# 64-row turns with shared banks, and a written-out order for all engines, in a lightning-attention and highway-FFN kernel

**Chip and metric.** One core of one Trainium2 chip. The time is device microseconds of one execution. "Fast" and "slow" are the two states in which executions fall; only fast runs are compared, and where a slow run or a slow profile is shown, it is said.

## The reference

Linear attention with a decay per head, in blocks of 64 tokens, then a highway feed-forward layer over all heads:

```python
# q, k, v: (4, 8, 768, 64) float32, lam: (8,), w_h, w_t: (512, 512), b_t: (512,)
for b in range(nb):                       # blocks of 64 tokens
    intra = einsum('bhic,bhjc->bhij', qb, kb) * Dmask      # lam ** (i - j), i >= j
    intra = einsum('bhij,bhjd->bhid', intra, vb)
    inter = einsum('bhid,bhde->bhie', qb * lam_pow, kv_state)
    out[:, :, sl] = intra + inter
    kv_state = lam_block * kv_state + einsum('bhsd,bhse->bhde', kb * rev_pow, vb)
x = out.transpose(0, 2, 1, 3).reshape(3072, 512)
H = maximum(x @ w_h, 0)
T = 1 / (1 + exp(-(x @ w_t + b_t)))
return T * H + (1 - T) * x                # float32, (3072, 512)
```

## The kernel before

It works in 12 stages of 256 tokens (J = 2 times 128 rows). In each stage k and q are loaded, scaled and turned, so that the head dimension lies on the partitions; scores, masks, state and output follow in 64x64 tiles; the feed-forward blocks come out transposed, and the result is turned back. The loads are issued by SyncE. Three functions concern us (the first serves k and q; the comments are mine):

```python
def trans(x, n, p, hs):              # k and q: 8 turns of 128 rows by 128 columns a group
    for i, h in enumerate(range(hs.start, hs.stop, 2)):
        for j in range(J):
            T.transpose(get(x + "tr", n, p)[:, i, j, :], get(x + "b", n)[:, j, h:h + 2, :], id128)
...
def block(x, w, g, js):              # feed-forward: 8 matmuls with 256 columns a call
    for i, j in enumerate(js):
        for kc in range(KC):
            T.matmul(get(x, g, js[0])[:, i, :], lhsT=w[:, kc, j * 128:(j + 1) * 128], rhs=get("xT", g)[:, kc, :],
                     start=(kc == 0), stop=(kc == KC - 1))
...
def turn(n, b, p, js):               # output: x + th, turned back; 8 turns of 128 rows
    g, r = group(n, b)
    for j in js:
        for i, x in enumerate(("xT", "th")):
            T.matmul(get("x", n, b, p)[:, (j - js[0]) * 128:(j - js[0] + 1) * 128],
                     lhsT=get(x, g)[:, j, r * C:(r + 1) * C], rhs=id128,
                     start=(j == js[0] and i == 0), stop=(i == 1), skip_group_check=True)
```

All of these write to tiles with the tag "w", which has three PSUM banks. Each piece of work is a task with an engine, a duration and a priority. At build time a planner simulates the engines and makes the order; among TensorE's candidates it ranks like this:

```python
k = (max(0.0, s - free[e] - GAP), (t.key if t.key > -9 else 99) + SAME * (t.mode != last_mode) + WAIT * (s - free[e]))
```

## Time and profile before

| | before |
|---|---|
| time, median of 3 | 116.28 us (115.97 to 116.59) |
| span in the trace | 113.2 us |
| TensorE busy | 101.2 us, 2145 matmuls in the trace |
| ScalarE / GpSimd / VectorE busy | 76.5 / 69.6 / 67.7 us |
| DMA | full until about 82 us |

TensorE is the bound in the middle, so the table is read from the top: another engine's busy time matters only where TensorE waits for it. The prediction below shows the lines. One line of the same page that it does not show turns out to be the important one, the queue that brings the instructions (packets, MB, share of the 16 DMA engines):

```profile
q8 instruction: 16, 0.26, 1.0%
```

(This trace, of 113.2 us, is of a fast run that took 115.21 us.)

### The profile page before, as it was taken

What the parts mean: (1) busy time and instruction counts of PE and PEld (TensorE: products, weight loads), DVE (VectorE), ACT (ScalarE), POOL (GpSimd) and SP (SyncE); (2) the same over time, 40 slices, a digit from 0 to 9 for tenths busy, and PEclk for the clock granted to TensorE, in tenths of its full rate; (3) what the DMA queues carried; (4) which work ended last, traced back from release to release, by engine and by line L of the source; (5) the groups of instructions that cost most, each with busy time, mean ns of one, the idle gap of its engine ahead of it and who ended that gap; (6) DMA issues with size and microseconds to landing.
All of it is one profiled execution on the core that took longest, in us unless ns stands there. A gap on an engine that the chain in (4) does not pass through costs nothing.

```text
span 113.2 us, 4880 instructions
## 1 busy us (share of the span) xinstructions
PE 101.2 (89%) x2145; PEld 88.9 (78%) x2145; DVE 67.7 (60%) x113; ACT 76.5 (68%) x146; POOL 69.6 (61%) x61
## 2 busy tenths in 40 slices
PE   4896576998897999999999999999999999998860
PEld 4895364778686788989889898998998989888750
DVE  0237756475266759658495676774966749764420
ACT  3595681556877676694879686967878667377550
POOL 6032337238999987979997997969597300404220
PEclk9999996799999999999999999999999999999999
DMA  0999999999999999999999999999951040403154
GB/s 9 255 298 291 311 329 349 302 263 300 279 296 291 336 352 306 293 288 298 307 320 310 285 340 294 333 285 298 337 184 53 11 180 6 184 7 148 37 208 162
DMA packets 43484, 27.57 MB, mean 243 GB/s; under 512 B 1348, under 2 KB 40520, under 8 KB 43464
## 3 DMA queue, kind: packets, MB, share of 16 engines
q1 hardware_dynamic: 43312, 27.27, 84.4%
q8 instruction: 16, 0.26, 1.0%
q14 instruction: 4, 0.03, 0.1%
q10 hardware_dynamic: 152, 0.01, 0.1%
HBM read 20.98 MB, written 6.29 MB: 241 GB/s over the span
## 4 chain that ended last, share of the span: by engine, by line
PE 72%; SPq 8%; DVE 7%; DMA 5%; ACT 3%; issue 2%; POOLq 1%; ACTq 0%
PE w L422 37%; PE w L444 9%; PE w L355 8%; SPq L341 7%; PE o L396 6%; DMA vf<-in_v_dram 5%; PE s L371 5%; PE o L384 5%; PE kv L404 4%; DVE m L375 3%; ACT w L435 2%; DVE xT L306 2%; DVE th L438 1%; SPq L300 1%; POOLq L602 1%
## 5 line engine op out<-in xcount | busy, mean ns | idle before, releaser
L422 PE MATMUL w<-xT,w_b 128*128 128x256 bf16 (+1 forms) x416 | 47.8, 267 | 1.4 <-DVE th L438 0.9
L422 PEld LDWEIGHTS <-w_b 128*128 128x128 bf16 x416 | 37.1, 99 | 6.5 <-issue 1.9
L375 DVE TENSOR_TENSOR m<-s,tri 128x512 bf16<-128x512 f32 x48 | 31.6, 686 | 14.7 <-PE s L371 14.7
L438 POOL TENSOR_TENSOR th<-t_sb,hmx 128x512 bf16<-128x512 bf16 (+1 forms) x13 | 14.0, 1080 | 21.2 <-DVE hmx L426 14.8
L349 POOL TENSOR_TENSOR qb<-qf,pow_q 128x1024 bf16<-128x1024 f32 (+1 forms) x13 | 22.1, 1703 | 7.8 <-DMA qf<-in_q_dram 7.7
L426 DVE SCALAR_TENSOR_TENSOR hmx<-w,xT 128x512 bf16<-128x512 f32 (+1 forms) x26 | 16.8, 647 | 10.0 <-PE w L422 5.2
L349 POOL TENSOR_TENSOR vs<-vf,pow_k 128x1024 bf16<-128x1024 f32 (+1 forms) x11 | 20.1, 1824 | 2.3 <-DMA vf<-in_v_dram 2.3
L450 ACT ACTIVATE o_sb<-w 128x512 f32<-128x512 f32 (+1 forms) x24 | 13.6, 587 | 5.3 <-PE w L444 5.0
L435 ACT ACTIVATE w<-w,bt_col 128x256 f32<-128x256 f32 (+1 forms) x26 | 11.2, 432 | 8.3 <-ACT kT L304 4.0
L304 ACT ACTIVATE qT<-w 128x1024 bf16<-128x1024 bf16 (+1 forms) x14 | 12.7, 904 | 4.8 <-PE w L355 4.8
L306 POOL CAST kb<-kf 128x1024 bf16<-128x1024 f32 (+1 forms) x11 | 11.0, 997 | 6.3 <-DMA kf<-in_k_dram 6.3
L304 ACT ACTIVATE kT<-w 128x1024 bf16<-128x1024 bf16 (+1 forms) x14 | 12.6, 896 | 1.9 <-PE w L355 1.9
L444 PE MATMUL w<-id,th 128*128 128x128 bf16 x96 | 12.9, 219 | 0.6 <-POOL th L438 0.6
L444 PE MATMUL w<-id,xT 128*128 128x128 bf16 x96 | 13.0, 220 | 0.4 <-DVE th L438 0.4
L438 DVE TENSOR_TENSOR th<-w,hmx 128x512 bf16<-128x512 f32 (+1 forms) x13 | 8.4, 645 | 6.3 <-ACT w L435 6.3
L435 ACT ACTIVATE t_sb<-w,bt_col 128x256 bf16<-128x256 f32 (+1 forms) x26 | 10.5, 461 | 2.4 <-PE w L422 2.4
L371 PE MATMUL s<-qT,kT 64*64 64x128 bf16 x384 | 11.4, 219 | 0.3 <-DVE m L375 0.3
L404 PE MATMUL kv<-vs,kb 64*64 64x64 bf16 x320 | 9.5, 197 | 1.3 <-POOL vs L349 0.9
L444 PEld LDWEIGHTS <-th 128*128 128x128 bf16 x96 | 9.3, 98 | 1.4 <-POOL th L438 0.8
L413 ACT ACTIVATE ss<-kv 128x256 bf16<-128x256 f32 x20 | 7.7, 384 | 3.5 <-PE kv L404 3.5
L404 PEld LDWEIGHTS <-kb 64*64 64x64 bf16 x320 | 8.0, 111 | 2.4 <-issue 1.6
L444 PEld LDWEIGHTS <-xT 128*128 128x128 bf16 x96 | 9.2, 98 | 0.5
(43 smaller groups left out, 109.2 us busy)
## 6 DMA issues: line engine op xcount, KB each, us to landing
out_dram<-o_sb SPq DMA_DIRECT2D x23, 256.0 KB, 4.9
kf<-in_k_dram SPq DMA_DIRECT2D x10, 512.0 KB, 7.5
qf<-in_q_dram SPq DMA_DIRECT2D x10, 512.0 KB, 7.8
vf<-in_v_dram SPq DMA_DIRECT2D x10, 512.0 KB, 7.0
kf<-in_k_dram SPq DMA_DIRECT2D x4, 256.0 KB, 5.2
qf<-in_q_dram SPq DMA_DIRECT2D x4, 256.0 KB, 5.7
vf<-in_v_dram SPq DMA_DIRECT2D x4, 256.0 KB, 6.1
w_f<-in_moe_w_h_dram SPq DMA_DIRECT2D x4, 256.0 KB, 6.2
```

Source lines behind the costliest of these rows:

```text
L304: A.activation(dst, src, AF.Copy)
L306: ENG[eng].tensor_copy(dst, src)
L349: ENG[eng].tensor_tensor(dst[:, hs], in0=get(x, n, p).rearrange("p h (j d) -> p h j d", j=J), in1=pw[:, :, :, None].to_broadcast([128, hs. ...
L371: T.matmul(get("s", n, u)[half(b), e, i, j, :], lhsT=get("kT", n)[half(e), hp, j, half(b)], rhs=get("qT", n)[half(e), hp, b * C:(b + 1) * ...
L375: V.tensor_tensor(get("m", n, u)[:, e], in0=get("s", n, u)[:, e], in1=tri[:, None].to_broadcast([128, 2, J, C]), op=ALU.mult)
L404: T.matmul(get("kv", n // NST)[half(e), hp, :], lhsT=get("kb", n)[half(b), j, 2 * hp + e, :], rhs=get("vs", n)[half(b), 2 * hp + e, j, :], ...
L422: T.matmul(get(x, g, js[0])[:, i, :], lhsT=w[:, kc, j * 128:(j + 1) * 128], rhs=get("xT", g)[:, kc, :], start=(kc == 0), stop=(kc == KC - 1))
L426: V.scalar_tensor_tensor(get("hmx", g, js[0]), in0=get("h", g, js[0]), scalar=0.0, in1=get("xT", g)[:, js[0]:js[-1] + 1, :], op0=ALU.max, ...
L435: A.activation(get(*gate(g, js))[:, i, :], get("t", g, js[0])[:, i, :], AF.Sigmoid, bias=bt_col[:, j:j + 1])
L438: ENG[TH[js[0] // 2]].tensor_tensor(get("th", g)[:, js[0]:js[-1] + 1, :], in0=get(*gate(g, js)), in1=get("hmx", g, js[0]), op=ALU.mult)
L444: T.matmul(get("x", n, b, p)[:, (j - js[0]) * 128:(j - js[0] + 1) * 128], lhsT=get(x, g)[:, j, r * C:(r + 1) * C], rhs=id128, start=(j == ...
L450: A.activation(get("o_sb", n, b, p), get("x", n, b, p), AF.Copy)
```

## The change

The intent is to make the turns cheaper. A turn of 128 rows by 128 columns becomes two turns of 64 rows by 64 columns, side by side in the two row halves of the array. Each group writes two banks, one for each row tile; k and q of a stage share these two, and so do the two halves of an output. Everything else is rearranged around that: the planner is gone, a list of 538 numbers gives the order of all tasks, and strings give the engine of each copy.

```diff
-def plan(tasks):
- ... (the whole planner, its durations and keys)
+EN = dict(cw="GVVGGVGV", ck2="AAAA", ..., ss="AAAAAAVVAAVVVAVVAVAV", eo="AAAVAAAAAAAAAAAVAAVAAV",
+          ck="GGGAGGGGGG", cq="VGGGGGGGGG", cv="VGGGGGGGGG", ...)
+ORDER = [44, 54, 20, 2, 21, 22, 23, 46, 24, ..., 520, 536, 537]
 ...
+    def trans2(i, n):
+        for hp in range(NP):
+            for j in range(J):
+                for b in range(2):
+                    T.transpose(get("tr", n, b)[:, i, hp, j, :], get("kq"[i] + "b", n)[half(b), j, 2 * hp:2 * hp + 2, :], id128[half(b), half(b)])
+    def evac2(n, b, eng):
+        copy(eng, get("kqT", n)[:, :, :, b * C:(b + 1) * C].rearrange("p x n (q j) -> p x n q j", j=J),
+             get("tr", n, b).rearrange("p x n j q -> p x n q j"))
 ...
+    def turn2(n, bs=(0, 1)):
+        for b in bs:
+            for j in range(NP):
+                for i, x in enumerate(("xT", "th")):
+                    for e in range(2):
+                        T.matmul(get("x", n, "e", e)[:, b, j, :], lhsT=get(x, n)[half(e), j, b * C:(b + 1) * C], rhs=id128[half(e), half(e)],
+                                 start=(b == 0 and j == 0 and i == 0), stop=(i == 1), skip_group_check=True)
 ...
-    for t in plan(tasks):
-        t.emit()
+    for i in ORDER:
+        t = tasks[i]
+        assert all(d in issued for d in t.deps)
+        issued.add(t)
+        t.emit(t.eng)
```

k and q of stages 2 to 11 and the output of stages 0 to 10 take the new form, 42 groups in all. The scores of the two halves of a head pair also get tiles of their own.

## The prediction

> **What bounds the kernel now.** I read the page first (busy shares and the 40 slices), then the groups of matmuls by form, the chain that ended last in order of time, and the timeline around single hand-overs.
>
> The page:
>
> ```profile
> PE 101.2 (89%) x2145; PEld 88.9 (78%) x2145; DVE 67.7 (60%) x113; ACT 76.5 (68%) x146; POOL 69.6 (61%) x61
> PE   4896576998897999999999999999999999998860
> POOL 6032337238999987979997997969597300404220
> PEclk9999996799999999999999999999999999999999
> DMA  0999999999999999999999999999951040403154
> ```
>
> TensorE is at 9 from slice 14 (about 40 us) to about 105 us. GpSimd is nearly full too, and the DMA is full, but only until about 82 us: both run ahead of TensorE and then stop. The clock dips only around 18 to 22 us. So the span is: a start in which the loads decide (0 to some 28 us), a long middle in which TensorE decides, and a tail. 113.2 us in this trace stand for 116.28 us of device time; I convert by that ratio.
>
> The matmuls by form (busy, mean ns, idle before):
>
> ```profile
> L422 PE MATMUL w<-xT,w_b 128*128 128x256 bf16 x352 | 43.8, 276 | 1.0 <-DVE xT L306 0.4 <-DVE th L438 0.4
> L444 PE MATMUL w<-id,xT 128*128 128x128 bf16 x96 | 13.0, 220 | 0.4 <-DVE th L438 0.4
> L444 PE MATMUL w<-id,th 128*128 128x128 bf16 x96 | 12.9, 219 | 0.6 <-POOL th L438 0.6
> L404 PE MATMUL kv<-vs,kb 64*64 64x64 bf16 x320 | 9.5, 197 | 1.3 <-POOL vs L349 0.9 <-ACT ss L413 0.4
> L355 PE MATMUL w<-id,qb 128*128 128x128 bf16 x96 | 7.7, 220 | 1.0 <-POOL qb L349 1.0
> L355 PE MATMUL w<-id,kb 128*128 128x128 bf16 x96 | 7.7, 219 | 1.2 <-DVE kb L306 1.2
> L384 PE MATMUL o<-qT,ss 64*64 64x128 bf16 x160 | 7.4, 227 | 0.2 <-DVE xT L306 0.2
> ```
>
> The mean of about 220 ns is latency; matmuls overlap. What one costs in a stream has to come from the chain, where one period of the middle reads:
>
> ```profile
> 70.62 0.57 PE o L396 x32
> 71.19 0.22 PE s L371 x16
> 71.42 0.24 PE kv L404 x16
> 71.66 0.55 PE w L355 x8
> 72.22 1.75 PE w L422 x16
> 73.96 0.45 PE w L444 x8
> 74.41 0.45 PE o L384 x12
> ```
>
> The rates follow by division. A feed-forward matmul (256 columns) costs 1.75/16 = 109 ns, a turn by 128 columns 0.45/8 = 56 ns. The 64x64 groups: scores 0.22/16 = 14 ns, so four in 56; the state update with 64 columns 0.24/16 = 15, so a pair in 30. A turn right after a 64x64 group costs 0.55 instead of 0.45. The starts of single matmuls show it too:
>
> ```profile
> 66.62 0.22 PE L444 MATMUL w<-id,th 128*128 128x128 bf16 x1
> 66.77 0.52 PE L384 MATMUL o<-qT,ss 64*64 64x128 bf16 x12
> ```
>
> Here the start-to-start distance is 149 ns, where 56 is normal: 93 ns for a change of tile shape. I find the same 93 to 95 ns at most of the 48 changes after 19 us, in both directions. Changes are dear in this kernel: two cost what three turns cost.
>
> [...] In the trace two full 128x128 loads start as little as 15 ns apart, so two of them would fit in 30 ns; that they do with 64 rows is not shown by this trace. [...]
>
> **The change, part by part.** (a) Turns. Eight 128-row turns with 128 columns (0.45 us) become 16 with 64 rows and 64 columns, two row tiles side by side: 8 pairs x 30 ns = 0.24 us. That holds for k and q in stages 2 to 11 (20 groups) and for the output in stages 0 to 10 (22 groups): 42 x 0.21 = 8.8 us less TensorE time. The first two stages and the last output stay as they were.
>
> (b) Changes of shape. The turns shared the 128x128 shape with the feed-forward blocks; now they have a third one (64x128). I numbered the tasks in the order in which the program makes them and read the list as an order for TensorE. From the first feed-forward block on it has 79 changes; the kernel before has 48 after its first block. 31 x 0.093 = 2.9 us come back. So a third of what (a) saves is lost.
>
> (c) What is left for TensorE after the first feed-forward block. Before: blocks 42.0, turns of the output 10.8, of k and q 9.0, intra 4.9, scores 4.7, state 4.1, inter 4.3, changes 4.5: 84.2 us. It took 91.2 (18.6 to 109.8): 7 us of cold clock, waits and tail on top. After: blocks 42.1, turns 5.3 + 0.9 and 4.3, intra 5.0, scores 4.5, state 4.1, inter 3.8, changes 7.4: 77.3.
>
> (d) The start, where the loads decide. From GpSimd's waits on loads:
>
> ```profile
> 20.63 0.61 POOL L306 CAST w_b<-w_f 128x512 bf16<-128x512 f32 x1 [1.47 <-DMA w_f<-in_moe_w_h_dram]
> 23.96 1.04 POOL L306 CAST kb<-kf 128x1024 bf16<-128x1024 f32 x1 [2.72 <-DMA kf<-in_k_dram]
> ```
>
> About 4.6 MB had to be loaded for the first and 5.8 for the second, which fits a landing at 5.2 us + MB/0.305. In the new list the last weight quarter comes after k, q and v of stage 2, with 6.8 MB loaded: it lands at about 27.6 and is cast by 28. TensorE's order puts the block that needs it eighth from its first block, with 73.0 us of work behind it. The kernel before has at 28 us: 109.8 - 28 = 81.8, less about 4.4 us of later waits and tail, so 77.4 of work. The advance is thus only about 4.4 us, not the 5.9 of (a) less (b).
>
> (e) GpSimd gives the cast of k in stage 5 and the scalings of stage 2 to ScalarE and VectorE, some 5 us, all early. ScalarE gives about 8 state copies (0.38 each), a few output copies (0.6) and one copy of 1.02 to VectorE: about 6 us move, ScalarE near 71, VectorE near 74. Neither becomes the bound by its sum.
>
> (f) Stores move behind the loads: eight stores stand before the last load, where the kernel before had twelve. That makes the loads end at about 80 instead of 82 us.
>
> (g) Sum: the same extras and tail, 4.4 us less: span 108.8, times 116.28/113.2 = 111.8. I put 111.6, as list and engine choices look tuned to the waits that I counted as unchanged.
>
> **Rivals.** *Weight loads bind the pairs.* If a load of 64 rows by 128 columns is not fast, or two of them do not overlap, a pair costs about 56 ns as before. (a) then gives nothing, (b) still costs 2.9, and the time is 117 to 120. For it: 128 weight columns now stand against only 64 moving columns. Against it: the 15 ns between two full loads. I give it 10%.
>
> *GpSimd and the loads become the bound.* GpSimd needs 1.04 + 1.90 + 1.90 + 1.15 = 6.0 us a stage, the loads 1.57 MB/0.305 = 5.2 plus stores; TensorE's stage falls from 7.4 to about 6.8. I walked down GpSimd's order with the landing times of (d): q of stage 11 is scaled at about 85 us. TensorE wants it at 28 + 73.0 - 16.8 = 84, 16.8 being its work from the last turns of k and q. So the two meet, and a loss of a few us on this side shows directly: 112 to 114.5. I think some of it likely (25%).
>
> *Two banks at a time starve the blocks.* Three banks serve the blocks, the turns and the output; a turn takes two of them, and its second half waits for a 1.02 us copy. Walking one stage (7 to 9) through the list, I found every bank free 0.2 to 1 us before its use, so by the list it does not stall. If the copies slip, 0.3 us a stage cost 3 us, and the gain is mostly gone.
>
> *A better start than I think.* If the new order fills the early gaps (5 us of idle TensorE between 10 and 20 us), the advance is nearer 6 to 7 us: 109.
>
> **Range and chances.** The middle case gives 111.6. Upwards 3 us of bank or load stalls make 114.6, downwards a full 7 us make 109; with some room for the tail the range is 108.2 to 114.6. The line of 2% is 113.95, which the stalls would have to eat half of the gain to reach: 0.78 faster, 0.18 within, 0.04 slower (the first rival).
>
> **What would show it.** Right: in the chain a turn group of 16 takes about 0.24 us (0.33 with a change of shape); starts of pairs are 30 ns apart; about 90 changes of shape in all, 93 ns each, the new shape too; TensorE at its last weight quarter at about 28 us; its busy time falls by less than the turns save. Wrong: pairs at 56 ns; a change to 64x128 that costs nothing or far more than 93; TensorE idle before feed-forward blocks with VectorE or ScalarE as releaser over 3 us in total; turns of k or q that wait for GpSimd over 2 us in the middle.

## The result, and the profile after

| | before | after |
|---|---|---|
| median, same chip | 116.12 us (114.79 to 116.59, 4 runs) | 122.53 us (121.94, 121.95, 123.10 fast; 124.43 slow) |
| ratio of fast runs | | 1.0575 [1.0428, 1.0723] |
| TensorE busy / span | 101.2 / 113.2 | 102.8 / 122.7 |

The ratio is the mean time of one kernel's fast runs over that of the other's in the same rounds, so it is not quite the ratio of the medians. The predicted 111.6 us, and its range, were missed by far, and to the other side: the change costs about 6.5 us.

The profile of the changed kernel fell on the slow run. The profile of experiment e2 below, of a fast run, shows the same thing in a smaller amount: 7.6 us of the standstills that are described here, where this one has 9.1. The page (TensorE with its matmuls, then the 40 slices, then the instruction queue):

```profile
PE 102.8 (84%) x2481; PEld 83.9 (68%) x2481; DVE 75.2 (61%) x126; ACT 73.9 (60%) x136; POOL 64.9 (53%) x58
PE   5992789979899898947599959599999999998870
PEclk9999558999999999999859995899999999999998
DMA  0999999999999999999999999402840020194754
q8 instruction: 19, 0.31, 1.0%
```

A slice is 3.07 us. TensorE has holes from 52 to 61 us, at 71 and at 77, where before it was at 9 throughout. Its clock drops to half twice in the middle, for 3.4 us each, from 60.5 and from 74.1 us. There are 336 more matmuls, each with its weight load, so 672 more instructions (42 groups x 16), and three more instruction packets.

What TensorE waits for in the changed kernel (line, releaser, us in total, times, longest):

```profile
PE s L249 <- issue: 3.4, 2, 2.1
PE w L300 <- issue: 2.4, 2, 1.8
...
PE kv L282 <- issue: 1.8, 2, 1.0
PE o L274 <- issue: 1.5, 1, 1.5
...
PE w L233 <- POOL kb L176: 0.3, 1, 0.3
```

9.1 us of waiting are put down to "issue": TensorE waited for nothing that the profile knows. The same view of the kernel before has no line of that kind among its waits. And the wait for GpSimd in the middle, which I had feared, is 0.3. The chain of the changed kernel in order of time (start, duration) shows where they lie:

```profile
51.88 0.76 PE w L300 x6
52.64 1.80 issue
54.44 0.39 PE w L300 x2
...
55.19 0.57 PE w L332 x32
...
56.57 0.57 PE w L233 x32
57.14 0.34 PE s L249 x14
57.49 2.06 issue
59.54 0.24 PE s L249 x2
59.79 2.84 PE w L300 x16
62.62 1.00 PE o L274 x32
```

The standstill stands after 6 of the 8 matmuls of a feed-forward call, and after 14 of the 16 of a score group. The program has no reason to wait at such places: the seventh matmul reads the same tiles as those before it. After the second standstill the clock fell: 16 feed-forward matmuls take 2.84 us instead of 1.75, and 32 of intra 1.00 instead of 0.57.

### What all standstills have in common

I counted TensorE's matmuls and weight loads from its first one, in order of time. The standstills of the changed kernel (gaps of over 0.5 us from 20 us on) fall at instructions 702, 1470, 1726, 1982, 2238, 2750 and 3006. Each of these numbers is 190 more than a multiple of 256. The instruction queue's packets have 16,384 bytes each, 19 of them in this run, where TensorE has 4,962 instructions, 19.4 times 256. If a packet holds 256 instructions, that is 16,384 / 256 = 64 bytes for one (an estimate from these counts). So I took the standstills to be at borders between blocks of instructions. Here are twelve of the block fetches (eight of 19 after the change, four of 16 before), from the times of the packets and of the matmuls about each border. A gap is from the start of the last matmul to the start of the first (us):

```
changed kernel: packet of 16,384 bytes    last matmul      first matmul     gap
                start      end            before border    after border
                40.59      41.78          42.15            43.15            1.00
                46.04      47.08          47.64            48.52            0.88
                52.02      52.98          52.37            54.44            2.08
                57.03      58.13          57.27            59.54            2.27
                62.32      63.35          68.21            68.24            0.03
                70.42      71.52          71.44            73.13            1.69
                77.06      78.15          78.03            79.60            1.57
                84.16      85.09          89.86            89.86            0.00
before:         40.13      41.15          42.80            42.91            0.11
                50.78      51.82          55.22            55.33            0.11
                66.56      67.71          71.08            71.09            0.00
                79.68      80.78          82.28            82.32            0.03
```

Wherever there is a standstill of over 0.5 us, TensorE goes on 2.42 to 2.71 us after the packet's start: about 1.1 us for the packet, and 1.4 to 1.6 after its end. The kernel before has its tightest borders at 2.63 and 2.77 us (82.32 and 42.91): it just got through. So my theory after the result was: **TensorE's instructions come too late**; a block is fetched only after the border before it has been passed, and if TensorE passes its 256 instructions faster than the fetch takes, it stands still. The rivals: late data that the profile does not name; something in the new order, by chance at these places; the new tile shape itself; the stores or the depth of the DMA queue.

### The profile page after: what moved, and what is told of

Its sections match the earlier page's. It is cut to its first block, busy times and chain, and to the rows that moved or that the text cites.

```text
span 122.7 us, 5537 instructions
## 1 busy us (share of the span) xinstructions
PE 102.8 (84%) x2481; PEld 83.9 (68%) x2481; DVE 75.2 (61%) x126; ACT 73.9 (60%) x136; POOL 64.9 (53%) x58
## 4 chain that ended last, share of the span: by engine, by line
PE 60%; SPq 16%; issue 9%; DMA 6%; ACT 4%; DVE 3%; POOLq 1%
PE w L300 33%; SPq L208 11%; DMA w_f<-in_moe_w_t_dram 6%; PE s L249 6%; SPq L170 5%; PE w L332 5%; PE w L233 4%; PE o L274 4%; PE kv L282 4%; PE o L262 4%; ACT w L313 3%; DVE th L316 2%; ACT o_sb L174 1%; POOLq L503 1%; ACT xT L174 0%
## 5 line engine op out<-in xcount | busy, mean ns | idle before, releaser
L216 POOL TENSOR_TENSOR qb<-qf,pow_q 128x1024 bf16<-128x1024 f32 (+1 forms) x11 | 19.2, 1747 | 13.6 <-DMA qf<-in_q_dram 13.6
L174 ACT ACTIVATE kqT<-w 128x1024 bf16<-128x1024 bf16 x19 | 18.7, 1023 | 4.7 <-PE w L233 4.6
L249 PE MATMUL s<-kqT 64*64 64x128 bf16 x320 | 10.3, 230 | 3.4 <-issue 3.4
L174 ACT ACTIVATE xT<-o 128x512 bf16<-128x512 f32 x16 | 9.1, 596 | 3.4 <-PE o L274 3.0
L274 PE MATMUL o<-m,vs 64*64 64x128 bf16 x384 | 9.3, 234 | 1.6 <-issue 1.5
L249 PEld LDWEIGHTS <-kqT 64*64 64x64 bf16 x320 | 6.7, 112 | 5.0 <-issue 4.7
L176 POOL CAST kb<-kf 128x1024 bf16<-128x1024 f32 x9 | 9.3, 1037 | 0.7 <-DMA kf<-in_k_dram 0.7
L199 PE MATMUL o<-id 128*128 128x128 bf16 x96 | 8.0, 258 | 1.4 <-POOL id masks.py:199 1.4
L274 PEld LDWEIGHTS <-vs 64*64 64x64 bf16 x384 | 6.9, 116 | 3.2 <-issue 3.0
L199 PEld LDWEIGHTS <-id 128*128 128x128 bf16 x96 | 7.4, 120 | 1.6 <-POOL id masks.py:199 1.4
```

The costliest lines, as they stand in the source:

```text
L174: A.activation(dst, src, AF.Copy)
L199: T.matmul(get("fill")[:, 0, i, :], lhsT=id128, rhs=id128, start=True, stop=True)
L216: ENG[eng].tensor_tensor(dst[:, hs], in0=get(x, n, p).rearrange("p h (j d) -> p h j d", j=J), in1=pw[:, :, :, None].to_broadcast([128, hs. ...
L249: T.matmul(get("s", n, u, e)[half(b), i, j, :], lhsT=turned("k", n)[half(e), hp, b * C + j:(b + 1) * C:J], rhs=turned("q", n)[half(e), hp, ...
L274: T.matmul(get("o", n)[half(e), b, 2 * u + i, :], lhsT=get("vs", n)[half(b), 4 * u + 2 * i + e, j, :], rhs=get("m", n, u)[half(b), e, i, j ...
```

## The experiments

All are correct but e3. Its output is wrong, which doesn't matter for the time. "Standstills" are gaps at block borders. F in the expectations is the theory above.

### e1: the same list with 128-row turns

```diff
-                for b in range(2):
-                    T.transpose(get("tr", n, b)[:, i, hp, j, :], ...[half(b), j, 2 * hp:2 * hp + 2, :], id128[half(b), half(b)])
+                T.transpose(get("tr", n, i)[:, hp, j, :], get("kq"[i] + "b", n)[:, j, 2 * hp:2 * hp + 2, :], id128)
 ...
-                    for e in range(2):
-                        T.matmul(get("x", n, "e", e)[:, b, j, :], lhsT=get(x, n)[half(e), j, b * C:(b + 1) * C], ...
+                    T.matmul(get("x", n, "e", b)[:, j * 128:(j + 1) * 128], lhsT=get(x, n)[:, j, b * C:(b + 1) * C], rhs=id128, ...
```

> The changed kernel with its list, its engines and its banks, but the turns of k, q and the output done as 128-row turns by 128 columns again (half as many instructions for them; correct result). Theory F (instruction supply): TensorE's program is fetched in blocks of 16 KB, that is 256 instructions, and with the DMA full a block comes too late for a program this dense; with some 4,290 instead of 4,960 instructions the standstills at block borders (8.1 us in six of them in the changed kernel) go, while the turns cost 7.8 us more: 117 to 119 us, no standstill over 0.6 us that has no releaser. Rival W (a wait on a bank or an engine that the new list brings and the profile does not name): the standstills stay at the same groups, and the dearer turns come on top: 127 to 130 us.

Measured: 120.09 us (118.95 to 120.66, all fast) against 115.89 of the kernel before on the same chip, ratio 1.0403 [1.0341, 1.0466]. No standstill. TensorE's instructions are again 4,290, as before the change. So the order and the engines are the same as in the changed kernel and the standstills are gone: the list alone does not make them. But all that is left of the change without the new turns (the order, the engines, the tiles shared by two turns; "the list" below) costs some 4.6 us by the ratio. That is a second finding: of the two halves of this change, one is a loss by itself.

### e2: 64 more matmuls at the start

```diff
-        for i in range(4):
+        for i in range(8 if len(fills) <= 16 else 4):     # the warm-up matmuls
```

> The changed kernel with 64 more warm-up matmuls (128 instructions) in the first 5 us, where TensorE waits for loads; nothing else is touched. F: the standstills stay at an instruction count of 190 modulo 256, and so come 64 matmuls earlier in the work than before, in other groups of the list; in all 6 to 9 us again, time 120 to 124 us. W: they stay at the same matmuls of the same stages, which now have a count of 62 modulo 256.

Measured: 121.96 us (fast) and 125.02 (slow). The standstills are at instructions 1726, 1982, 2238, 2494 and 3006, again 190 more than multiples of 256, though everything in the work now comes 128 instructions later. They took 1.1 to 2.3 us, 8.0 in all (four gaps of 0.3 to 0.6 us lie at other borders), and hit other groups of the list. If data or the order made them, they would have moved with the work. They stayed with the count. The profile fell on the fast run.

### e3: no loads after stage 5

```diff
+    def alias(x, n, p):
+        made[x, n, p].obj = made[x, 2 + n % 4, p].obj     # an older stage's tile in place of a load
 ...
+   ... (lambda eng, x=x, n=n, p=p: alias(x + "f", n, p)) if n >= 6 else (the load)
```

> Wrong result on purpose: the changed kernel without the loads of k, q and v from stage 6 on, whose tiles are read from older stages; every engine's work is the same. The DMA is then idle from about 45 us on but for stores. F: standstills at block borders only up to about 45 us (at most 1.5 us in all); the rest of TensorE's work runs through, 109 to 113 us. W: they stay, 118 us or more.

Measured: 113.30 us (113.05 and 113.55), ratio 0.980 [0.9726, 0.9874]; relative error 0.996, as intended. TensorE's largest wait for "issue" in its profile:

```profile
PE kv L285 <- issue: 0.3, 1, 0.3
```

The standstills vanish, all but two gaps of about 0.4 us at 37.8 and 43.1, where loads still ran. It was not the loads' data that TensorE had waited for: in the changed kernel it waits 0.3 us for a cast of k in this stretch, and for no other product of a load. What the loads do is to fill the DMA (the page of the changed kernel has it at 90% or more in every slice from 3 to 77 us). From the first matmul after a border to the start of the next fetch it takes 2.2 to 3.9 us in the changed kernel between 31 and 78 us, and at most 1.5 us in e3 after 47 us, as in both other kernels once their loads are over. And TensorE without standstills passes 8 of its last 12 blocks here in 2.9 to 4.2 us, where the kernel before never took less than 4.3. With 2.5 us from the start of a fetch to its use, there is room for a delay of 0.4 to 1.7 us. With the loads running, the fetch does not keep that.

### e4: stores moved forward between the loads

The edit is in the numbers of the list: each store task of stages 0 to 9 moves to 8 places behind the copies of its output. The trace has 12 stores ahead of the last load then, as in the kernel before, and 8 in the changed kernel; the 14 of the expectation is a miscount.

> The changed kernel with each store of stages 0 to 9 moved up to shortly after its output copy, between the loads, as in the kernel before (14 instead of 8 stores ahead of the last load). If the fetch is late because the loads stand two or three deep in front of it, mixing in stores lets it start sooner: standstills under 4 us in all, 116 to 119 us. If only the density of the program counts, they stay at 6 us or more and the time at 121 to 124 us.

Measured: 124.37 us (122.25, 123.14 fast; 125.61, 127.07 slow), ratio 1.0612 [1.0522, 1.0702]. Gaps of 0.98, 0.70, 1.18, 2.65 and 2.08 us, 7.6 in all against 9.5 of the six in the table above, and the time is no better. So where the stores stand does not decide whether standstills come. I had wondered whether the smaller number of stores between the loads makes the DMA fuller for the fetches; this speaks against it.

### e5: the kernel before with more instructions

The counter-test: nothing of the change, but each feed-forward matmul of 256 columns as two of 128. The stream grows by about 1 us, the instructions from 4,290 to 4,994, about as many as in the changed kernel.

```diff
-            for kc in range(KC):
-                T.matmul(get(x, g, js[0])[:, i, :], lhsT=w[...], rhs=get("xT", g)[:, kc, :], ...)
+            for r in range(2 if g < N - 1 else 1):
+                for kc in range(KC):
+                    T.matmul(get(x, g, js[0])[:, i, r * C:(r + 1) * C], lhsT=w[...], rhs=get("xT", g)[:, kc, r * C:(r + 1) * C], ...)
```

> The kernel before, its list and its turns, with each feed-forward matmul of 256 columns given as two of 128 (704 instead of 352, each with its weight load): TensorE's instructions rise from 4,290 to 4,994, as many as the changed kernel has, while its stream gets only 352 x 3 ns = 1 us longer; no new bank, shape or list; correct result. F: 256 instructions now pass in some 4.6 us of a stage instead of 5.4, and standstills at block borders appear between 30 and 82 us, 4 to 9 us in all: 120 to 126 us. Rival (what stands still in the changed kernel has to do with its tiles or its list): no standstills, 116 to 118 us.

Measured: 123.02 us (121.92, 122.33, 123.72 fast; 124.11 slow) against 117.05 (the median of twelve runs, six of them slow), ratio of fast runs 1.0567 [1.0455, 1.068]. That it equals the loss of the change, 1.0575, almost to the digit is chance: there the list costs time and the turns save some. TensorE's waits and a piece of its chain (the profile is of a slow run):

```profile
PE w L445 <- issue: 2.4, 2, 1.6
PE kv L404 <- issue: 2.0, 2, 1.6
```

```profile
44.86 0.21 PE kv L404 x5
45.07 1.61 issue
46.68 0.28 PE kv L404 x6
```

The standstills of 1.80, 1.57, 1.80 and 1.05 us stand at 187 or 188 more than multiples of 256 (a few records are probably missing). Here there is no new shape, no list, no bank change. More instructions in the same work are enough. The rival of the new tile shape falls.

### e6: at most two loads in flight

```diff
+            if len(flying) >= 2:     # a DMA of 4 bytes that reads the load before last, ahead of each load
+                nc.sync.dma_start(out=pk_ln[...], in_=flying[-2][0:1, 0, 0:1])
+            flying.append(get(x, n, p))
```

> The changed kernel with at most two loads of k, q and v in flight from stage 2 on (the queue waits for the last but one load by a copy of 4 bytes out of its tile before it issues the next); correct result. If a fetch is late because it stands behind three or four loads of 512 KB, it now starts some 2 us sooner, and the standstills at block borders fall under 3 us in all; the loads lose 5 to 10% of their rate, which GpSimd may feel: 115 to 120 us. If the depth does not matter: standstills of 6 us and more, 121 us or above.

Measured: 133.32 us, ratio 1.1381. The intention failed: with so few loads in flight the DMA was no longer full (mostly 5 to 8 tenths busy from 33 us on) and the loads became the bound; TensorE waited for v through GpSimd (the longest waits of its profile, a slow run):

```profile
PE kv L289 <- POOL vs L223: 8.5, 3, 5.5
```

Standstills at borders of 1.60, 0.58, 0.97 and 1.03 us remained. A miss: it does not tell how the depth of the queue bears on the fetch. But a DMA that is full throughout is not needed for a standstill. What counts is the moment of the border, as all 14 traces together show (borders after 19 us, DMA share of loads and stores within 0.5 us of the first matmul after the border): at the 52 borders with a share under 5% the next fetch started 1.2 us after the border at the latest; at the 135 with over 90% it was 2.2 us in the median and up to 4.1.

### e7 and e10: 64-row turns in the planner of before

If the list costs 4.6 us and the fetches the rest, the turns might gain in the old planner. e7 uses them in all stages, e10 only for k and q from stage 10 and for the output from stage 8, when the loads are nearly over. The diff is that of the change for `trans2`, `evac2` and `turn2`, with a threshold:

```diff
+TR64, X64 = 2, 0          # e7;  10, 8 in e10
+        T64 = n >= TR64
+            if T64:
+                for i, (x, c1) in enumerate((("k", ck), ("q", cq))):
+                    task("PE", 0.24, n - K[x], lambda i=i, n=n: trans2(i, n), mode=2, ...)
```

> The 64-row turns with two banks shared (stages 2 to 11, output 0 to 10), put into the kernel before with its own planner and engine choices in place of the written list; correct result. F: the program is as dense as in the changed kernel, so standstills at block borders of 4 to 9 us in all, whatever the list: 114 to 121 us. If the list is what brings the standstills: none, 109 to 112 us.

> The kernel before with its planner, where only the late turns are in 64-row tiles: the output from stage 8 on and k and q from stage 10 on, after nearly all loads have landed; correct result. F: no standstills, and a saving of 5 x 0.42 us less some 5 changes of shape of 0.09: 1.5 us, ratio 0.98 to 0.995. If 64-row tiles do harm in themselves (banks, changes): 1.0 or above.

Measured: e7 129.97 us (126.60 its only fast run), e10 118.84 (117.58, 118.23, 118.72, 118.96 fast; 119.41 and 120.62 slow), ratio of fast runs 1.0199 [1.0114, 1.0283]. Both missed what I expected, e7 by my own fault: I kept the planner's priorities, which place k and q of a stage far apart. As the two now share two banks, these are held all that time, and in its turns of k and q TensorE waits for the copies of k and q, 4.3 us (4 times) in e7 and 1.1 us once in e10. e7 has standstills besides (2.16 us at 55.8 and 2.14 at 67.1 us), e10 has none. Neither says what a well-placed version is worth.

### e12: only the late outputs, at the planner's places

```diff
+TR64, X64 = 99, 8
```

> The kernel before with its planner, with only the output's turns of stages 8, 9 and 10 in 64-row tiles (after the loads), k and q untouched, and the turn placed where the planner had it: correct result. The tiles save 3 x 0.42 us and add some 5 changes of shape of 0.093: 0.8 us, ratio 0.985 to 1.0, no standstill at a block border. (The late variant before this one lost 2%: there the planner turned k and q of one stage far apart and so held two banks.)

Measured: 117.66 us (116.38, 116.51, 117.34, 117.99 fast; two slow), ratio 1.0101 [1.0039, 1.0163]. No standstills, and no gain: about 1% slower, just outside what I expected, and I did not look for the reason. Three outputs can save at most 6 x 0.21 us less their changes of shape, so no more than "nothing gained" can be read from it.

### e13: e1 with 64 more warm-up matmuls

```diff
-        for i in range(4):
+        for i in range(8 if len(fills) <= 16 else 4):     # on top of e1
```

> The changed list with 128-row turns (as e1_turn128) and 64 more warm-up matmuls at the start. In e1_turn128 TensorE idles 1.8 and 1.3 us at 9 to 12.5 us and its clock then is at half speed for 10 us; here it should stay up. If this cold spell is a part of what the list loses: 118 to 119 us, 1 us under e1_turn128. If the loads alone decide the start: 120 us as there.

Measured: 118.54 us (117.81 to 118.82), ratio 1.018 [1.0136, 1.0225]; e1 had 1.0403, on another chip. The clock row of e1 and then that of e13:

```profile
PEclk9999955579999999999999999999999999999999
```

```profile
PEclk9999999999999999999999999999999999999999
```

With the list TensorE is idle at the start, its clock is halved for some 10 us (from 14.6 to 24.8), and with 64 matmuls on nothing it stays up. They are worth 1.5 us by the medians and 2.6 by the ratios; the two profiles differ by only 0.5 us (117.2 and 116.7), so the size is not sharp. Part of what the list costs is this cold spell. Another part is that it changes between the 128x128 and the 64x64 shape more often than the planner's order: I count 71 changes after 19 us in e1, 48 in the kernel before. 23 x 0.093 = 2.1 us, an estimate from these counts and the measured change.

### e14: 64-row turns for k and q only

The edit is the output's half of e1's, on the changed kernel: 4,610 instructions.

> The changed kernel with 64-row turns for k and q only and 128-row turns for the output: 4,611 instructions, between the 4,290 of e1_turn128 and the 4,963 of the changed kernel; correct result. F: the standstills at block borders lie in between, 1 to 5 us in all, and what the tiles save (3.5 us) is about eaten up: 118 to 121 us. If the standstills belonged to the output's tiles alone: none, 116 to 117; to those of k and q alone: 8 us, 124 or more.

Measured: 119.41 us (118.64, 119.16, 119.67 fast; 122.05 slow), ratio 1.0243 [1.019, 1.0296]. TensorE's waits in its profile:

```profile
PE w L233 <- issue: 0.8, 1, 0.8
PE w L331 <- issue: 0.7, 1, 0.7
PE o L274 <- issue: 0.6, 1, 0.6
```

2.1 us of "issue", where the changed kernel has 9.1 and e1 none, and all at 190 more than multiples of 256. The standstills follow the instructions by dose: 4,290, 4,610 and 4,962 instructions give 0, 2.1 and 9.1 us (the last in a slow run; 7.6 in the fast one of e2).

### e11: fewer instructions

If instructions are scarce, take some away. In the kernel before, VectorE adds xT to th, so that the output needs one turn in place of two: 88 turns, so 176 instructions, fewer, and 88 x 0.056 = 4.9 us less of TensorE.

```diff
+    def add_x(g):
+        V.tensor_tensor(get("th", g), in0=get("th", g), in1=get("xT", g), op=ALU.add)
 ...
-            for i, x in enumerate(("xT", "th")):
+            for i, x in enumerate(("th",)):            # but in the last stage
```

> A try at beating both: the kernel before with its planner, where VectorE adds xT to th (one addition of 1,024 bf16 columns a stage, stages 0 to 10), so that the output's turn needs one matmul per 128 columns instead of two: 88 matmuls and 176 instructions fewer on TensorE (4,115), 88 x 56 ns = 4.9 us less of its stream, and a program less dense, not more; correct result up to one more rounding to bf16. If TensorE's stream sets the time: 111 to 113 us. Against it: VectorE gets some 7 us more[...]: then 115 to 119 us.

Measured: 116.20 us (115.78 to 116.73 fast, one slow) against 116.48, ratio 0.9985 [0.9945, 1.0025]: the same. The additions (busy, mean ns) and what TensorE waits for:

```profile
L441 DVE TENSOR_TENSOR th<-th,xT 128x1024 bf16<-128x1024 bf16 x11 | 11.6, 1055 | 0.6 <-POOL th L438 0.6
```

```profile
PE w L355 <- POOL qb L349: 2.5, 4, 0.7
PE o L396 <- DVE m L375: 2.1, 3, 1.0
```

An addition takes 0.69 us in the median but up to 2.38, and VectorE's masks come later: 2.1 us of waiting for them where the kernel before had 0.6, and 2.5 on GpSimd where it had 1.0. These two waits have grown by 3.0 us, so most of the 4.9 us is eaten by engines that were nearly full; the rest I did not trace. No correct version of mine beats the kernel before.

## Why the prediction was wrong

Step by step, as it was put:

- **(a) the turns: right.** The chain shows groups of 32 half-size turns at 0.57 us, that is twice 0.24 and one change of shape. In the profile after:

```profile
L332 PE MATMUL w<-id,xT 64*128 64x64 bf16 x176 | 7.0, 191 | 0.0
```

  The mean of 191 ns is latency again; pairs start 30 ns apart. Without loads (e3) the changed kernel is 6.8 us faster than its twin with 128-row turns (e1), where 8.8 less eleven or so extra changes of shape, 1.0, were to be expected; e3 has no late loads to wait for besides, so this is a rough check.
- **(b) the changes of shape: right.** From the first feed-forward block on I count 79 in the trace after, as forecast (88 in all), most of them at 93 ns, for the new shape too.
- **(c) the sum: right, as far as it can be read.** Its two sums are 0.1 us short of their parts. From the first feed-forward block to the last matmul e3, without standstills, takes 84.2 us (24.1 to 108.4), 6.9 more than the 77.3 forecast; the kernel before took 7 more than its sum.
- **(d) the start: nearly right.** The block with the last weight quarter starts at 28.88 us, not 28, and some 1 us of the advance is gone.
- **(e), (f): no consequence.** ScalarE has 73.9 and VectorE 75.2 us, and TensorE waits 1.0 us in all for th and 0.2 for a mask of VectorE after the start. (f) was wrong: the last load is issued at 85.5 us, not earlier but later than the 77.9 of the kernel before, yet TensorE does not wait for it; e4 shows that the stores' places do not decide.
- **(g) failed: "the same extras and tail".** I carried over the 7 us of cold clock, waits and tail and asked of each new wait whether an engine or a load could cause it. The standstills (9.1 us in the slow run, 7.6 in the fast one of e2) have neither as their cause. They are fetches of instructions. Of the 10.4 us between the predicted 111.6 and the 121.95 of the middle fast run, the standstills with the cold clock behind them are about 8.7 by an estimate (121.95 less the 113.3 of e3, which has no late loads to wait for either), and the rest I put down to the later block of (d) and a little more waiting. The conversion is loose too: the trace of 113.2 us is of a run of 115.21 us, so by that run a span of 108.8 stands for 110.8 and not 111.8.
- **The rivals failed too.** Weight loads did not bind (a pair of row tiles, with its two loads, takes 30 ns), and GpSimd took 0.3 us in the middle. Of the twelve waits in the profile one is for a bank: 1.0 us for th, whose work frees the bank of a block, 0.8 of it in the tail; the kernel before had 0.9. None of them named the supply of instructions, and my list of what would prove me wrong looked for releasers only.

What I should have done is to count: (a) doubles the instructions of 42 groups and makes them pass in half the time. A turn group goes from 16 instructions in 0.45 us to 32 in 0.24. The kernel before passes its borders, one every 256 instructions, without a loss (0.11 us at most at those in the table); the changed one stands still for up to 2.27 us at one, 9.1 us in all of 122.7.

**Shown:** standstills go with the count (e2), need no part of the change (e5), go when the loads go (e3), grow with the number of instructions (e1, e14), and fetches start late where the DMA is busy (all traces: 1.2 us after the border at the latest with a share under 5%, 2.2 us in the median and up to 4.1 with over 90%). **Inferred:** that the passing of a border starts the next fetch, from the order of the times alone: of the 19 fetches of the changed kernel, 18 start after the first matmul behind a border, each before the next one is reached, and one 0.6 us ahead of that matmul. **Open:** why the fetch starts later in the changed kernel (2.2 to 3.9 us after a border between 31 and 78 us) than in the one before (0.4 to 3.1 us between 34 and 80), though the DMA is equally full in both. e4 and e6 were to tell, and did not. Open also is up to 1 us of what the list costs.

## What to carry to other kernels

Cutting matmuls into smaller ones that run side by side took a turn group here from 0.45 to 0.24 us, and from 16 instructions to 32: before you count such a gain, divide 256 instructions, the distance of the borders here, by the rate at which TensorE will pass them, and compare it with the tightest border of the kernel that you have (here TensorE passed it 2.63 us after the start of the packet, and where it stood still, it went on after 2.42 to 2.71). Where a profile shows TensorE idle with "issue" and no releaser, in the middle of a group, number its instructions and look whether the places repeat at a fixed distance, here 256. And test a bundled change by halves: here all but the turns cost some 4.6 us, which a good result of the turns would have hidden.
